# Splitting a buffer fill round the second square root and moving two small steps of a decode kernel

## The chip, the cores and the metric

The kernel runs on one core of a Trainium2 chip. The metric is device time in microseconds. A profile's span (first to last instruction) is 1.3 to 1.6 us shorter than the measured time of the same run.

Names of the profile: PE does matrix products (PEld is its loading of weights), DVE vector work, ACT activation functions, POOL memsets here, and SP issues the loads. PSUM is the memory that PE writes to. A line of a timeline has start and length in us, engine, source line, instruction, what it writes and reads, shapes, count, and in brackets the idle time before it with what ended it. A landing record is the time at which a load's semaphore tells that one of the 16 transfer engines is done with it.

## The reference

One decode step: four batch rows, width 448, 16 query heads on 8 key/value heads, 8192 cached positions of 256. The attention is gated by a small MLP whose output goes through silu. Cut to what matters:

```python
xn = _layernorm(x)
s  = attention(xn, k_cache, v_cache, wq, wo)   # caches: 4 x 8 x 8192 x 256, bf16, read once
xn2 = _layernorm(xn)                           # second layernorm: inside the MLP
# (with one position per row the four shifted groups are zero, so w1 and w2 drop out)
h2 = _gelu(xn2 @ w3) @ w4
return x + s * _silu(xn + h2)
```

The two caches are 268 MB of the 279 MB that are read.

## The kernel before

The work is a loop over 16 pairs of (row, key head). In each round PE turns keys (K), DVE and ACT copy them out of PSUM, PE forms scores, and the value product (PV) of the *previous* pair is done at the end of the round. Round 0 has no previous pair, so its PV runs on a value buffer that must hold finite numbers. At the start that buffer carries the weights wq and w3, and ACT fills what they leave free with zeros:

```python
def prog_act(act):
    ...
    for k, col in ((1, 0), (2, 8)):                  # the two layernorms' square roots
        act.wait_ge(S["v_w"], k)
        c(act.activation(st[:, col + 2:col + 3], st[:, col + 1:col + 2], ACT.Sqrt))
    act.wait_ge(S["g_c"], NPC)                       # POOL's memsets, of pT too
    for t in (vflat[1][:, DK * HDH:NCH * DH], vflat[0][:, DK * FH:NCH * DH]):
        c(act.activation(t, pT[:, 0:1].broadcast_to([P, t.shape[1]]), ACT.Copy))
    act.wait_ge(S["v_w"], 3)
    c(act.activation(gel_b[:, :], gel_a[:, :], ACT.Tanh))
```

DVE then waits for that tanh and ends gelu, before it copies any keys. All loads go through SP's queue. It asks for the next keys when a half of the key buffer has been copied out:

```python
if i > 0:
    sp.wait_ge(S["v_k"], NVK * (i - 1) + 1 + t)
```

At the end the last pair's values come in five pieces and wo's last heads in four. PE's order there:

```python
for i in range(NPIECE - ND):                 # value pieces 0, 1, 2
    take(pe, "dvl%d" % i, 16)
    ins = f_pv(kv, PIECES[i], PIECES[i + 1], pb)
ins.then_inc(S["p_pv"], 1)
take(pe, "v_a")
for i in range(NDG):                         # o's first sums
    pe.matmul(o_ps[i * PQ:(i + 1) * PQ, 0:DQ], selb[:, :],
              ou_f[:, i * DQ:(i + 1) * DQ], start=True, stop=False)
f_direct(NPIECE - ND)                        # piece 3
take(pe, "v_po")
...                                          # sums of pieces 0 to 2, piece 4
take(pe, "dwl0", 16)
f_o(LATE[0])                                 # then the other wo pieces, each when it lands
```

## Time and profile before

| | before |
|---|---|
| median of the first 3 runs | 653.08 us (652.23 to 653.20) |
| span of the profiled run | 651.4 us |
| PE, DVE, ACT busy | 77%, 40%, 41% |
| the queue's transfers | 278.99 MB, 99.5% of 16 engines' span |
| last weights (wo) complete | 648.55 us |

One line of the DMA queue's own timeline: when SP asks for the second pair's keys (columns: start, length, the instruction).

```profile
40.08 12.98 SPq L249 DMA_DIRECT2D kn<-in_A_k_cache_dram  x3
```

### The profile page before, as it was taken

Reading aid. Unit: us, or ns where it says so; the run is one execution under the profiler, and the core shown is the slowest. Engines: PE = TensorE matmul, PEld = TensorE weight load, DVE = VectorE, ACT = ScalarE, POOL = GpSimd, SP = SyncE. Lnnn points to the kernel's source line nnn. Section 1 sums busy time; section 2 is a strip of 40 time slices with the busy share of each in tenths; the row PEclk is TensorE's granted clock in tenths of the full one; section 3 lists DMA queues with packets and bytes.
Section 4 is the critical chain, followed back from the end, with each engine's and each line's share of the span. In section 5 each row is a group of like instructions: output and inputs, shape, how many; then the busy total and the mean of one; then the engine's idle time right before and its main releaser. Section 6 shows DMA issues by size and latency. Waiting matters only on the chain. (4 is left out here: it accounts for less than half of the span.)

```text
span 651.4 us, 22029 instructions
## 1 busy us (share of the span) xinstructions
PE 500.4 (77%) x9695; PEld 411.7 (63%) x9695; DVE 257.4 (40%) x507; ACT 268.5 (41%) x360; POOL 3.7 (1%) x18
## 2 busy tenths in 40 slices
PE   2898989685876958589587867969588595958956
PEld 1794969384673938558285764938467393855924
DVE  7343535252452524335153442525245252433511
ACT  3752636163451615436044542616345161543610
POOL 2000000000000000000000000000000000000000
PEclk9587989797996969889698997969789797988978
DMA  9999999999999999999999999999999999999997
GB/s 385 439 419 430 431 439 441 427 447 423 440 447 404 461 408 457 412 435 453 412 450 417 457 423 425 441 429 445 425 441 447 404 457 412 461 408 435 453 405 301
DMA packets 10641, 279.13 MB, mean 429 GB/s; under 512 B 1028, under 2 KB 3080, under 8 KB 3592
## 3 DMA queue, kind: packets, MB, share of 16 engines
q1 hardware_dynamic: 10616, 278.99, 99.5%
q8 instruction: 7, 0.11, 0.1%
q14 instruction: 2, 0.02, 0.0%
q10 hardware_dynamic: 16, 0.01, 0.0%
HBM read 278.99 MB, written 0.00 MB: 428 GB/s over the span
## 5 line engine op out<-in xcount | busy, mean ns | idle before, releaser
L651 PE MATMUL pst<-ident_b,kn 128*128 128x128 bf16 x4096 | 304.2, 222 | 26.5 <-PEq L317 24.9
L351 ACT ACTIVATE kT<-pst 128x1024 bf16<-128x1024 bf16 x224 | 226.1, 1023 | 119.1 <-ACTq L317 118.9
L349 DVE COPY kT<-pst 128x1024 bf16<-128x1024 bf16 x288 | 197.5, 691 | 175.4 <-DVEq L317 175.3
L651 PEld LDWEIGHTS pst<-ident_b,kn 128*128 128x128 bf16 x4096 | 241.2, 99 | 28.0 <-issue 28.0
L664 PE MATMUL psc<-qc,kT 128*128 128x4 bf16 x4096 | 174.5, 165 | 7.9 <-PEq L317 7.8
L664 PEld LDWEIGHTS psc<-qc,kT 128*128 128x128 bf16 x4096 | 154.4, 97 | 36.6 <-issue 36.1
L696 PE MATMUL psv<-vb,pT 128*8 128x512 bf16 x1024 | 102.3, 497 | 95.6 <-PEq L317 95.6
L372 ACT ACTIVATE pT<-psc,negb 64x128 bf16<-64x128 f32 x64 | 28.4, 535 | 237.2 <-ACTq L317 236.9
L696 PEld LDWEIGHTS psv<-vb,pT 128*8 128x8 bf16 x1024 | 24.6, 93 | 127.4 <-issue 116.5
L507 DVE TENSOR_REDUCE rmax<-psc 64x2 f32<-64x256 f32 x32 | 13.5, 423 | 134.4 <-DVEq L317 134.2
L689 PE MATMUL psm<-sel,po 128*128 128x4 f32 x136 | 19.2, 264 | 1.4 <-PEq L317 1.4
L689 PEld LDWEIGHTS psm<-sel,po 128*128 128x128 f32 x136 | 18.1, 204 | 1.5 <-issue 1.5
L372 ACT ACTIVATION_READ_ACCUMULATOR pT<-psc,negb 64x1 f32 x64 | 16.4, 256 | 0.0
L536 DVE COPY po<-psv 128x512 f32<-128x512 f32 x17 | 11.8, 692 | 9.5 <-DVEq L317 9.5
L528 DVE COPY negb<-psm 128x4 f32<-128x4 f32 x16 | 2.6, 162 | 28.3 <-DVEq L317 28.3
L517 DVE TENSOR_REDUCE gmax<-psm 2x2 f32<-2x128 f32 x16 | 4.5, 279 | 20.2 <-DVEq L317 20.2
L361 ACT ACTIVATE vb<-pT 128x2048 bf16<-128x2048 bf16 (+1 forms) x2 | 10.4, 5252 | 0.0
L677 PEld LDWEIGHTS psm<-diag,ones_f 2*128 2x128 f32 x32 | 4.7, 182 | 7.0 <-issue 7.0
L673 PEld LDWEIGHTS psm<-ident_f,rmax 128*2 128x2 f32 x16 | 1.3, 81 | 11.6 <-issue 11.6
L596 PE MATMUL pst<-ident_b,xn_b 4*128 4x4 bf16 x14 | 0.7, 162 | 9.6 <-DVE xn_b L421 9.5
L596 PEld LDWEIGHTS pst<-ident_b,xn_b 4*128 4x128 bf16 x14 | 0.5, 100 | 10.5 <-issue 9.5
L681 PE MATMUL psw<-rowsum,ones_f 128*128 128x4 f32 x34 | 6.8, 269 | 0.0
(93 smaller groups left out, 84.7 us busy)
## 6 DMA issues: line engine op xcount, KB each, us to landing
kn<-in_A_k_cache_dram SPq DMA_DIRECT2D x30, 4096.0 KB, 26.4
kn<-in_A_k_cache_dram SPq DMA_DIRECT2D x4, 2048.0 KB, 15.6
vb<-in_A_v_cache_dram SPq DMA_DIRECT2D x2, 4096.0 KB, 19.1
kn<-in_A_v_cache_dram SPq DMA_DIRECT2D x1, 4096.0 KB, 27.7
vb<-in_A_wq_dram SPq DMA_DIRECT2D x1, 3584.0 KB, 11.4
kn<-in_A_v_cache_dram SPq DMA_DIRECT2D x1, 2048.0 KB, 26.2
wo_sb<-in_A_wo_dram SPq DMA_DIRECT2D x1, 2016.0 KB, 40.9
vb<-in_B_w_dram SPq DMA_DIRECT2D x1, 1568.0 KB, 14.0
```

What stands on the lines that cost most here:

```text
L349: engine.tensor_copy(dst, src).then_inc(S["v_ev"], 1)
L351: engine.activation(dst, src, ACT.Copy).then_inc(S["a_ev"], 1)
L361: c(act.activation(t, pT[:, 0:1].broadcast_to([P, t.shape[1]]), ACT.Copy))
L372: ins = act.activation(pT[own, 0:NC2 * NR].rearrange("p (c n) -> p n c", n=NR)[:, n], psc[own, 0:NC2 * NR].rearrange("p (c n) -> p n c", n ...
L507: ins = v.tensor_reduce(rmax[own, :], psc[own, 0:NC2 * NR].rearrange("p (c n) -> p n c", n=NR)[:, t * REP:(t + 1) * REP], AX.X, ALU.max)
L536: v.tensor_copy(po[:, :], psv[:, 0:CP * DH]).then_inc(S["v_po"], 1)
L651: ins = pe.transpose(dst[:, n * P:(n + 1) * P], kn[:, t, GC * j + kl, half * P:(half + 1) * P], ident_b[:, :])
L664: ins = pe.matmul(psc[:, kk * NR:(kk + 1) * NR], kT[:, j % RING, n * P:(n + 1) * P], qc[:, :, half, :], start=(half == 0), stop=(half == N ...
L677: pe.matmul(psm[:, P:P + NR], ones_f[0:REP, :], diag[:, :], start=True, stop=True).then_inc(S["p_m2"], 1)
L681: pe.matmul(psw[:, 0:NR], ones_f[:, :], rowsum[:, :], start=True, stop=True).then_inc(S["p_s"], 1)
L689: ins = pe.matmul(psm[:, o:o + NR], po[:, i * DH + dh:(i + 1) * DH:NHALF], sel[:, i, 0:NR], start=(i == 0), stop=(i == CP - 1))
L696: ins = pe.matmul(psv[o:o + CP * NR, 0:CP * DH], pT[:, kk * NR:(kk + CP) * NR], src[:, kk:kk + CP, :].rearrange("p c d -> p (c d)"), start ...
```

## The change

The intent is to free ACT earlier, so that key copies start earlier, and to shorten PE's tail. It has three parts: the fill is split, with 5000 columns put in the idle gap between the square roots; gelu's end moves from the start into the half-time step of the MLP; o's first sums go from behind value piece 2 to behind piece 0. The semaphore that lets PE use the value buffer is now raised by ACT's fill. The core of the diff:

```diff
+            fills = ([vflat[0][:, DK * FH:DK * FH + FILL]],
+                     [vflat[0][:, DK * FH + FILL:NCH * DH], vflat[1][:, DK * HDH:NCH * DH]])
             for k, col in ((1, 0), (2, 8)):
                 act.wait_ge(S["v_w"], k)
                 c(act.activation(st[:, col + 2:col + 3], st[:, col + 1:col + 2], ACT.Sqrt))
-            act.wait_ge(S["g_c"], NPC)
-            for t in (vflat[1][:, DK * HDH:NCH * DH], vflat[0][:, DK * FH:NCH * DH]):
-                c(act.activation(t, pT[:, 0:1].broadcast_to([P, t.shape[1]]), ACT.Copy))
+                act.wait_ge(S["g_c"], NPC)
+                for t in fills[k - 1]:
+                    f = act.activation(t, pT[:, 0:1].broadcast_to([P, t.shape[1]]), ACT.Copy)
+            f.then_inc(S["dv"], 32)
 ... (DVE: the two steps behind "wait_ge(a_c, 5)" move to the head of f_mlp; its own
      sem_inc(dv, 32) goes; later counts on a_c are 2 lower) ...
                 for i in range(NPIECE - ND):
                     take(pe, "dvl%d" % i, 16)
                     ins = f_pv(kv, PIECES[i], PIECES[i + 1], pb)
+                    if i == 0:
+                        take(pe, "v_a")
+                        for n in range(NDG):
+                            pe.matmul(o_ps[n * PQ:(n + 1) * PQ, 0:DQ], selb[:, :],
+                                      ou_f[:, n * DQ:(n + 1) * DQ], start=True, stop=False)
                 ins.then_inc(S["p_pv"], 1)
-                take(pe, "v_a")
-                for i in range(NDG):
-                    pe.matmul(o_ps[i * PQ:(i + 1) * PQ, 0:DQ], selb[:, :],
-                              ou_f[:, i * DQ:(i + 1) * DQ], start=True, stop=False)
                 f_direct(NPIECE - ND)
```

More of the change, by code (lines that the diff above doesn't have):

```diff
@@ L130, in bass_recurrent_scan__gqa_block_cached__mixer_s_mlp__decode_kernel @@
     ROW_PAD = 192
+    FILL = 5000
     TW = NHALF * REP
@@ L459, in prog_dve @@
             v.sem_inc(S["v_po"], 1)
-            v.sem_inc(S["dv"], 32)
             v.wait_ge(S["g_c"], NPC)
@@ L483, in prog_dve @@
                           ).then_inc(S["v_q"], 1)
-            v.wait_ge(S["a_c"], 5)
-            c(v.tensor_scalar(gel_b[:, :], gel_b[:, :], 1.0, 0.5, op0=ALU.add, op1=ALU.mult))
-            c.sync()
-            v.tensor_tensor(hT[:].rearrange("p k a b -> p (k a b)"), gel_b[:, :], gel_u[:, :], ALU.mult
-                            ).then_inc(S["v_hT"], 1)
-            def f_mlp():
+            def f_mlp():
+                v.wait_ge(S["a_c"], 3)
+                v.tensor_scalar(gel_b[:, :], gel_b[:, :], 1.0, 0.5, op0=ALU.add, op1=ALU.mult
+                                ).then_inc(S["v_s"], 1)
+                take(v, "v_s")
+                v.tensor_tensor(hT[:].rearrange("p k a b -> p (k a b)"), gel_b[:, :], gel_u[:, :],
+                                ALU.mult).then_inc(S["v_hT"], 1)
                 take(v, "p_h2")
@@ L575, in prog_dve @@
             f_rz()
-            v.wait_ge(S["a_c"], 6)
+            v.wait_ge(S["a_c"], 4)
             c(v.tensor_scalar(sg4[:, :], sg4[:, :], 1.0, 0.5, op0=ALU.add, op1=ALU.mult))
```

## The prediction

> **What bounds the kernel now.** I read the page first (its busy shares, the slices, the queues), then the stretches around start and end, then the DMA queue's own timeline, then the engines' timelines at both ends. The page's slices and queue rows:
>
> ```profile
> DMA  9999999999999999999999999999999999999997
> q1 hardware_dynamic: 10616, 278.99, 99.5%
> ```
>
> The reader is to see that the transfers are busy in every slice while PE has 77% of the span, DVE 40% and ACT 41%. All data goes through one queue, 278.99 MB. To see whether the queue is ever short of work, I cut the span into stretches (columns: length, busy time of PE, PEld, DVE, ACT, POOL, clock, DMA share, GB/s):
>
> ```profile
> 0.00:2.00 2.00, 0.00 (x0) 0.00 (x0) 0.66 (x2) 0.90 (x1) 0.88 (x8) 1.00 0.92 229
> 2.00:20.00 18.00, 7.01 (x95) 4.32 (x95) 12.26 (x56) 8.38 (x5) 2.80 (x11) 0.96 0.97 412
> 20.00:24.00 4.00, 3.57 (x32) 3.33 (x32) 0.55 (x4) 3.98 (x2) 0.00 (x0) 0.50 1.04 442
> 24.00:40.00 16.00, 14.32 (x212) 14.35 (x213) 5.86 (x11) 7.33 (x9) 0.00 (x0) 0.53 0.98 413
> 40.00:60.00 20.00, 18.10 (x339) 12.97 (x339) 8.32 (x16) 7.06 (x7) 0.00 (x0) 0.83 1.03 431
> ...
> 648.60:651.40 2.80, 0.50 (x7) 0.22 (x4) 0.77 (x2) 0.00 (x0) 0.00 (x0) 1.00 0.01 1
> ```
>
> The DMA share is 0.97 to 1.04 from 2 us on, also at 20 to 24 us, where ACT is filling and PE is about to stall. From the transfer records I also summed the engines at work in every single microsecond: from 2 to 646 us it is never below 15 of 16. There is no hole to close. The DMA queue's own timeline shows the steady state:
>
> ```profile
> 491.06 11.28 SPq L249 DMA_DIRECT2D kn<-in_A_k_cache_dram  x2
> 516.23 0.33 SPq L249 DMA_DIRECT2D vb<-in_A_v_cache_dram  x1
> 529.74 11.27 SPq L249 DMA_DIRECT2D kn<-in_A_k_cache_dram  x2
> ```
>
> A pair starts every 529.74 - 491.06 = 38.68 us for four times 4096 KB, 16.78 MB, or 433.7 GB/s. Compute has time over in each such round; in the list of waits PE waits for values (the psv product) 97.4 us in 15 rounds, 6.5 us a round. What ends the span is the last rows of the timeline:
>
> ```profile
> 648.09 0.41 PEld L742 LDWEIGHTS pst<-wo_sb,OT_all 128*32 128x32 bf16 x8 [0.56 <-issue]
> 648.12 0.97 PE L742 MATMUL pst<-wo_sb,OT_all 128*32 128x224 bf16 x12 [0.37 <-PEq L317]
> 648.66 0.22 PEld L742 LDWEIGHTS pst<-wo_sb,OT_all 128*32 128x32 bf16 x4 [0.16 <-issue]
> 649.13 0.38 DVE L586 TENSOR_TENSOR res<-pst,sg 64x224 f32<-64x224 f32 x1 [2.90 <-PE pst L742]
> ```
>
> By the trace's landing records the last but one piece of wo is complete at 647.99 us and the last at 648.55. PE is idle before both, its loads starting 0.10 us after each. So the time is: about 1 us until the first data moves, 647 us of transfers without a hole, and 2.85 us of fixed work (651.40 - 648.55: four products, two DVE steps of 0.38 us, the store). The measured 653.08 is 1.3 to 1.7 us more than the profiled span.
>
> **What the Trainium skill says.** "DMA: Bandwidth & Descriptors", section "Specifications", gives a fabric ceiling of 435 GB/s beside an HBM limit of about 358 GB/s for one core. The trace agrees with the first (433.7) and not with the second as a bound for this run. There is nothing left in the rate. "ScalarE: Activation LUTs", section "Table sets: the hidden batching unit", says that copy is a filler in every set, so a copy between two square roots should need no new table. The trace agrees for the order it has: the fill starts at 12.31 us, straight after the second square root, without a load, and the only later load is the one ahead of tanh. Section "What ACT_TABLE_LOAD costs" gives about 1283 ns for the load; the trace has 1283 ns, with tanh starting 0.02 us after it, so no further drain shows here. It stays one load after the change.
>
> **Part 1, the fill split.** ACT's timeline at the start:
>
> ```profile
> 6.95 0.20 ACT L358 ACTIVATE st<-st 4x1 f32<-4x1 f32 x1 [4.56 <-DVE st L407]
> 12.21 0.20 ACT L358 ACTIVATE st<-st 4x1 f32<-4x1 f32 x1 [5.06 <-DVE st L407]
> 12.31 10.41 ACT L361 ACTIVATE vb<-pT 128x2048 bf16<-128x2048 bf16 x2
> 22.74 1.28 ACT L363 ACT_TABLE_LOAD   x1
> 24.04 0.25 ACT L363 ACTIVATE gel_b<-gel_a 128x56 f32<-128x56 f32 x1
> 24.31 1.02 ACT L351 ACTIVATE kT<-pst 128x1024 bf16<-128x1024 bf16 x1
> ```
>
> ACT idles 5.06 us between the roots and then fills for 10.41. By shape, 2048 columns take 1891 ns and 10112 take 8612, so 0.834 ns a column and 184 ns fixed. The first 5000 columns take 184 + 5000 x 0.834 = 4.35 us. They may start when POOL has ended its memsets (6.25 + 0.97 = 7.22 us) and end near 11.6, 0.6 us ahead of the second root at 12.21, which isn't delayed. The rest, 5112 and 2048 columns, takes 4.45 + 1.89 = 6.34 us: end at 18.65. Table load to 19.93, tanh to about 20.2 (its input is ready at 19.55 + 0.22 = 19.77). So ACT is free near 20.2 instead of 24.29. One more instruction, 0.18 us, lies in idle time.
>
> **Part 2, gelu's end to half time.** DVE now waits 3.73 us for tanh (24.32) before it empties the first score buffers at 24.84. Two instructions (0.19 + 0.22 us) and that wait leave the start. PE's first keys are turned from 20.11 to 23.68 us, at half clock 0.9 us a group of eight. DVE then empties group 0 near 21.1, ACT group 1 near 22, and PE's first score products can follow at 23.7 where they now start at 25.68: PE gains **2.0 us** there, no more, because the turning of keys becomes what it waits for. The next keys, asked for at 40.08 us, are asked for near 38. But the queue isn't empty at 40.08: the transfer ahead of it, wo, is complete on its first engine at 42.43 us and on its last at 44.51. A longer queue moves no byte sooner. **Worth on the span: 0.** At half time PE's half-way product has to wait for the two steps, some 0.6 us once. In steady rounds PE has 6.5 us over, and the next transfer is asked for over 20 us before it lands: also 0. (The residual copies already lie at half time in the old kernel; only gelu's end moves.)
>
> **Part 3, o's first sums ahead.** Four products of 352 ns, overlapped to 0.55 us, leave the stretch after the third value piece and go behind the first. There PE has idle time:
>
> ```profile
> 642.80 0.34 PEld L696 LDWEIGHTS psv<-kn,pT 128*8 128x8 bf16 x10 [2.26 <-issue]
> 643.26 0.33 PEld L772 LDWEIGHTS pst<-ou_f,selb 128*32 128x32 f32 x4
> 643.79 0.69 DVE L536 COPY po<-psv 128x512 f32<-128x512 f32 x1 [5.66 <-DVEq L317]
> 644.05 0.48 PEld L752 LDWEIGHTS pst<-pT,kn 128*128 128x128 bf16 x16 [0.46 <-issue]
> 644.60 1.02 PEld L778 LDWEIGHTS pst<-sel,po 128*128 128x128 f32 x8
> ```
>
> PE stands still about 2 us before the third piece (642.80), so 0.55 us fits there. But after it the L778 products need DVE's copy, which ends at 643.79 + 0.69 = 644.48 whichever way; they can't move. The L752 piece lands at 643.94 and starts at 644.05 already. So PE gains under 0.1 us by 645.85, and the wo pieces at 647.99 and 648.55 swallow that. **Worth: 0.**
>
> Sum: 0 + 0 + 0, with the median of before at 653.08 and its runs from 652.23. I take **652.9 us**, the middle of what these runs would give again, leaning a little low for the longer queue.
>
> **Rivals.** *The start counts in full:* if some executions that weren't profiled have a hole near 40 us (the queue has only 2.35 us left on its first engine there, and a first byte takes about 1 us), the earlier request would be worth up to 2.0 us: 651.1. For it: the margin is small, and before spreads over 1 us. Against it: no hole in the trace, and the profiled run is as slow as the others. *The end counts in full:* PE's tail shortens by 0.55 us, 652.5. Against it: PE is idle before both last pieces. *Slower, a new wait:* the first fill outlasts the gap and holds the second root, hence xn2 and the start of w3's products. It would have to be 0.6 us late to be felt at all, and some 4 us late to empty the queue at 40 us; or the half-time steps cost more than the 6.5 us that a round has over. Either would make 653 to 654. *The rate of the transfers changes* with a deeper queue or with ACT writing at another time: no term for it in the trace; 1 us either way.
>
> **Range and chances.** Three of the rivals lie within 2 us and the runs of one kernel within 1 us, so 651.2 to 654.4. Faster by 2% is 640 us, less than the bytes take at 433.7 GB/s (278.99 / 0.4337 = 643.3 us, plus 1 and 2.85 at the ends); only another count of bytes could do that. Slower by 2% needs 13 us of holes. Chances 0.01, 0.98, 0.01.
>
> **What would show it.** Right: the first fill of 4.35 us lies between the roots, tanh starts near 20, the first score products near 23.7, the second pair's keys are asked for near 38 instead of 40.08, and yet the rounds stay 38.68 us, the DMA share stays near 1 throughout and the last wo piece lands within 1 us of 648.55. L772 stands before 642.8 and L778 stays where it is. Wrong: the last landing moved by more than 1 us, or a microsecond with fewer than 15 engines at work in either kernel, or PE not idle before the last two wo pieces.

## The result, and the profile after

| | before | after |
|---|---|---|
| median of 6 runs each | 652.77 us (652.23 to 653.20) | 653.05 us (652.84 to 653.65) |
| ratio, 95% interval | | 1.0005 [0.9992, 1.0018]: same |
| profiled span | 651.4 us | 651.3 us |
| second pair's keys asked for | 40.08 us | 33.94 us |
| first score product | 25.68 us | 23.58 us |
| last wo piece complete | 648.55 us | 648.41 us |

The page's slices and queue rows of the changed kernel, and two of the stretches (columns as in the prediction):

```profile
DMA  9999999999999999999999999999999999999997
q1 hardware_dynamic: 10616, 278.99, 99.5%
```

```profile
2.00:20.00 18.00, 7.02 (x95) 4.33 (x95) 12.22 (x55) 12.67 (x8) 2.79 (x11) 1.00 0.96 409
20.00:24.00 4.00, 3.79 (x42) 3.82 (x43) 1.97 (x7) 1.28 (x3) 0.00 (x0) 1.00 1.03 438
```

Nothing moved for the transfers: the same bytes, the same share. (The share of a stretch counts a packet where it starts, so it can pass 1. The clock column reads 1.00 wherever the profile holds no clock record. The first record stands at 15.1 us in the kernel before and at 26.1 in this one, so the 1.00 of the second line is no measurement: the first 32 key products took 3.57 us in both kernels.) What moved is beside the transfers. Between 2 and 20 us ACT is busy 12.67 us instead of 8.38, and between 20 and 24 us 1.28 instead of 3.98, because part of the fill went into its gap. Its timeline at the start:

```profile
6.98 0.20 ACT L361 ACTIVATE st<-st 4x1 f32<-4x1 f32 x1 [4.60 <-DVE st L411]
7.29 4.37 ACT L364 ACTIVATE vb<-pT 128x5000 bf16<-128x5000 bf16 x1
12.25 0.20 ACT L361 ACTIVATE st<-st 4x1 f32<-4x1 f32 x1 [0.60 <-DVE st L411]
12.36 6.24 ACT L364 ACTIVATE vb<-pT 128x5112 bf16<-128x5112 bf16 x2
18.62 1.28 ACT L367 ACT_TABLE_LOAD   x1
19.92 0.25 ACT L367 ACTIVATE gel_b<-gel_a 128x56 f32<-128x56 f32 x1
22.20 1.02 ACT L352 ACTIVATE kT<-pst 128x1024 bf16<-128x1024 bf16 x1 [2.03 <-ACTq L318]
```

The reader is to see the second line, the fill between the roots, with 0.60 us of idle time left behind it, and the last line's wait of 2.03 us: ACT now stands ready for keys that PE hasn't turned yet. The SP request that answers to the 40.08 us of before:

```profile
33.94 16.74 SPq L250 DMA_DIRECT2D kn<-in_A_k_cache_dram  x3
```

It comes 6.14 us earlier and then waits in a longer queue. By the landing records that load of keys completes at 54.17 us on its last engine, and did so at 54.16 us before. The end of the changed kernel, after two lines of the kernel before for comparison:

```profile
642.83 0.81 PE L696 MATMUL psv<-kn,pT 128*8 128x512 bf16 x10 [1.78 <-PEq L317]
645.85 1.90 PE L742 MATMUL pst<-wo_sb,OT_all 128*32 128x224 bf16 x32
```

```profile
642.69 0.81 PE L700 MATMUL psv<-kn,pT 128*8 128x512 bf16 x10 [0.93 <-PEq L318]
643.65 0.69 DVE L540 COPY po<-psv 128x512 f32<-128x512 f32 x1 [5.26 <-DVEq L318]
643.91 0.48 PEld L756 LDWEIGHTS pst<-pT,kn 128*128 128x128 bf16 x16 [0.91 <-issue]
644.46 1.02 PEld L783 LDWEIGHTS pst<-sel,po 128*128 128x128 f32 x8
647.99 0.97 PE L746 MATMUL pst<-wo_sb,OT_all 128*32 128x224 bf16 x12 [0.38 <-PEq L318]
```

PE's wait ahead of the third piece shrank from 1.78 to 0.93 us. Its wait ahead of the last wo pieces is what it was, 0.38 us (0.37 before).

### The profile page after: what moved, and what is told of

Its sections match the earlier page's. It is cut to its first block, busy times and chain, and to the rows that moved or that the text cites. A ratio compares the mean times of both kernels' runs of the same rounds, so it can differ in the third digit from the quotient of the medians.

```text
span 651.3 us, 22030 instructions
## 1 busy us (share of the span) xinstructions
PE 501.3 (77%) x9695; PEld 409.0 (63%) x9695; DVE 257.2 (39%) x507; ACT 268.7 (41%) x361; POOL 3.7 (1%) x18
## 5 line engine op out<-in xcount | busy, mean ns | idle before, releaser
L700 PE MATMUL psv<-vb,pT 128*8 128x512 bf16 x1024 | 105.1, 506 | 99.6 <-PEq L318 98.7
L364 ACT ACTIVATE vb<-pT 128x5000 bf16<-128x5000 bf16 (+2 forms) x3 | 10.6, 3568 | 0.1
## 6 DMA issues: line engine op xcount, KB each, us to landing
wo_sb<-in_A_wo_dram SPq DMA_DIRECT2D x1, 2016.0 KB, 40.8
```

What stands on the lines that cost most here:

```text
L364: f = act.activation(t, pT[:, 0:1].broadcast_to([P, t.shape[1]]), ACT.Copy)
L700: ins = pe.matmul(psv[o:o + CP * NR, 0:CP * DH], pT[:, kk * NR:(kk + CP) * NR], src[:, kk:kk + CP, :].rearrange("p c d -> p (c d)"), start ...
```

## The experiments

The theory to be tested: the 279 MB in the queue set the time, the start of compute counts only if it lets the queue run dry, and PE's tail counts only beyond the idle time that it holds. The rivals: the start counts in full and something later gives it back; the tail counts in full; or compute sets the time and the change simply did nothing to it. In the runs below "before" was timed again in the same rounds: median 652.70 us for the first four, 652.77 for the next four, 652.80 for the last three.

### Each half of the change alone

```diff
 # e1_start_only: after.py with o's first sums back behind piece 2
 # e2_sums_only:  before.py with o's first sums behind piece 0
```

> Parts 1 and 2 alone (fill split, gelu's end at half time; o's first sums at their old place). Theory (the transfers set the time): ratio 1.000 within 0.002, last landing within 0.3 us of 648.5, although the second pair's keys are asked for 2 to 6 us before 40.08. Rival (the start counts and something later gives it back): 651 or 647, since the part that gives it back is not in this kernel.

> Part 3 alone (o's first sums behind the first value piece, start as in the old kernel). Theory: ratio 1.000 within 0.002; PE idle grows by about 0.5 us ahead of the fourth value piece and not at the end. Rival (PE's tail sets the end): 0.55 us less, 652.2. Also a second look at the old start: if half clock up to 38 us follows from PE's pause near 24 us, it is seen again here and not in the run of the start alone.

Measured: 652.88 us, ratio 1.0003 [0.9986, 1.0019], and 652.75 us, ratio 1.0000 [0.9984, 1.0017]. The start alone asked for the second pair's keys at 34.04 us and its last wo piece was complete at 648.37. So the sums don't give a gain back, since they aren't in that kernel. The half-time step still is in it, but it can't be what gives the gain back either: the load that was asked for 6 us earlier was complete at 54.03 us, against 54.16 before, and half time comes after 320 us. The gain was never one for the span. For the sums alone the times don't decide: the interval also holds the rival's 0.55 us less (0.9992). In the trace they gave nothing: the last wo piece was complete at 648.49 and PE's last wo product ended at 649.03 (648.55 and 649.09 before).

That trace also shows what I had not expected. By the clock records PE was at half clock from 635.1 to 641.9 us, where the kernel before has 636.3 to 639.8. It came to the wo products at 646.49 instead of 645.85 and did all 44 in 2.54 us without a wait. So how much PE has over at the end differs from run to run; in this one it was next to nothing.

### Bytes: half of one pair's values left out

```diff
 # e6_less_v: after.py with
-                    load(vv, src, 0, NC2, "dv")
+                    load(vv, src, 0, NCH if i == NPAIR - 2 else NC2, "dv")
```

This kernel is wrong: the second half of one pair's values is the pair before's. The check passed it all the same ("correct": true on record), so that check doesn't notice half of one pair's values.

> The changed kernel without the second half of the values of the last but one pair (wrong result on purpose): 4.194 MB less in the queue. Theory: 4.194 MB / 433.7 GB/s = 9.67 us less, 643.3. Rival (compute or a chain of waits sets the time): 653.

Measured: 643.31 us, ratio 0.9857 [0.9842, 0.9872], 9.46 us less than before (9.74 less than the changed kernel's 653.05). The queue's row of its page:

```profile
q1 hardware_dynamic: 10616, 274.80, 99.4%
```

With the compute untouched, the time follows the bytes at 4.194 MB / 9.46 us = 443 GB/s, 0.21 us short of the 9.67 that the steady rate gives. This shows directly what the profile's share suggested, and the rival of a compute bound falls.

### A later start: when does it begin to cost?

Extra fills of 5000 columns hold ACT, and with it the key copies. A semaphore of their own keeps the overlapping writes in order.

```diff
 # e3_old_fill1 (n = 1), e4_old_fill3 (n = 3): before.py, ahead of its fills
+            for i in range(n):
+                t = vflat[0][:, DK * FH:DK * FH + 5000]
+                act.activation(t, pT[:, 0:1].broadcast_to([P, t.shape[1]]), ACT.Copy).then_inc(S["xf"], 1)
+                act.wait_ge(S["xf"], i + 1)
 # e5_new_fill3 (n = 3), e9_new_fill1 (n = 1): after.py, the same behind its fills
```

> The old kernel with one more fill of 5000 columns ahead of its fills: ACT is free about 4.45 us later. Theory: a late start costs only the hole that it makes in the queue, request of the second pair's keys + 1.0 us to first data - 43.5 (mean end of the wo transfer over the engines). Request at 40.5 to 44.5, by PE's clock: cost 0 to 2.0 us, 652.8 to 654.8. Rival (the start counts in full): 4.45 us more, 657.2.

> The old kernel with three more fills of 5000 columns: ACT is free about 13.3 us later. Theory: request at 48 to 53.5, a hole of 5.5 to 11 us, 658 to 664, and the measured addition equals request + 1.0 - 43.5 within 0.7 us. Rival (the start counts in full): 666.1. Rival (start never counts): 652.8.

> The changed kernel with the same three more fills, behind its own: tanh would come near 33.3, the first ACT copy of keys near 33.5 instead of 22.2, 11.3 us later. Theory: request at 45 to 49, hole 2.5 to 6.5, 655.5 to 659.5, again request + 1.0 - 43.5 within 0.7 us; and 2 us or more below the old kernel with three more fills, so here, with the queue run dry, the change's start does count. Rival (start counts in full): 664.3. Rival (it never counts): 652.8.

> The changed kernel with one more fill of 5000 columns behind its own. The three runs with a hole put the knee at a request near 40.8 us (their profiled spans grew by request - 40.8, within 0.1). Here the first ACT copy of keys comes near 24.6 instead of 22.2, so the request for the second pair's keys comes at 36 to 40, short of the knee. Theory: 0 to 0.2 us more, 653.0, where the same fill in the old kernel cost 3.2. Rival (every us of a late start counts): 2.4 us more, 655.4.

| kernel | request | idle of the queue, 41 to 52 us | profiled span, and growth | median of runs (range) |
|---|---|---|---|---|
| before | 40.08 | 0 | 651.4 | 652.77 |
| before + 1 fill | 44.32 | 2.73 | 654.9, +3.5 | 655.86 (653.86 to 656.52) |
| before + 3 fills | 49.18 | 7.49 | 659.9, +8.5 | 665.67 (661.43 to 665.85) |
| after | 33.94 | 0 | 651.3 | 653.05 |
| after + 1 fill | 35.43 | 0 | 652.0, +0.7 | 653.11 (652.88 to 653.56) |
| after + 3 fills | 47.79 | 6.09 | 658.3, +7.0 | 659.11 (657.19 to 660.00) |

All in us; the idle time is the sum over the 16 engines divided by 16, from the transfer records. The request and the hole in the old kernel with one more fill, from the queue's timeline and from the stretches:

```profile
44.32 12.21 SPq L249 DMA_DIRECT2D kn<-in_A_k_cache_dram  x3
```

```profile
42.00:44.00 2.00, 2.00 (x42) 2.00 (x41) 0.89 (x2) 1.02 (x1) 0.00 (x0) 1.00 0.45 167
44.00:46.00 2.00, 1.69 (x47) 1.61 (x45) 0.94 (x2) 0.00 (x0) 0.00 (x0) 1.00 0.64 198
```

The same two stretches of the old kernel as it is:

```profile
42.00:44.00 2.00, 2.00 (x48) 2.00 (x46) 1.40 (x3) 1.77 (x2) 0.00 (x0) 1.00 1.30 533
44.00:46.00 2.00, 2.00 (x53) 2.00 (x51) 1.18 (x2) 1.48 (x3) 0.00 (x0) 1.00 0.92 395
```

The column before the last is the DMA share: 0.45 and 0.64 where the old kernel has 1.30 and 0.92. PE is busy 2.00 and 1.69 us against 2.00 and 2.00; the queue shows the loss far more. The mechanism holds: a lost microsecond of the queue never comes back in the following 600 us. The idle time makes up 2.73 of 3.5, 7.49 of 8.5 and 6.09 of 7.0 us. Most of the rest is transfers that took longer: summed over all records and divided by 16 they took 0.9, 1.0 and 0.6 us more than in the same kernel without extra fills. The size was off. I expected a growth of request + 1.0 - 43.5, that is 1.8, 6.7 and 5.3 us within 0.7, and found 3.5, 8.5 and 7.0: about 1.7 us more in each, a miss of my own stated width. For the kernel with one more fill three terms account for 1.5 of the 1.7. The wo data ended at 42.78 us in the mean and not at 43.5 (its landing records have 43.13 in that run, and a landing record comes some 0.35 us behind the data): 0.72. The first data followed the request by 0.96 to 1.80 us, by engine, 1.34 in the mean and not 1.0: 0.34. And each engine's first transfer after the hole took up to 1.94 us instead of 1.213, together 0.41. The remaining 0.2 I can't assign. What the runs say is simpler: the growth is the request less 40.8 us (3.5, 8.4 and 7.0). Carried back to no growth, which no run tests between 40.08 and 44.32, this line puts the old kernel's request at 40.08 only 0.7 us short of costing something.

The change moved it to 33.94. With one more fill the old kernel lost 3.2 us in the median and the changed one 0.06 over itself; with three, 665.67 stands against 659.11. **The change bought slack where there was no lack.** The ratios to before are 1.0037 [1.0018, 1.0055] and 1.0195 [1.0178, 1.0212] for the old kernel, 1.0004 [0.9989, 1.0019] and 1.0090 [1.0074, 1.0106] for the changed one; only the second is unclear at 2%, the others are the same. The old kernel's two medians lie above the ranges that I had stated. The other four runs of "before + 3 fills" lie 4 us above its profiled one (661.43), at what the rival of a full count had said (666.1). No profile shows their requests, so why is open, and in that row only the profiled run has request and span both known. What speaks against the full count is "after + 1 fill", where the same fill cost 0.06 us in the median. The +0.7 of "after + 1 fill" is no hole: the profiled run was that kernel's slowest, and its other runs had spans of 651.3 to 651.8. Its last wo piece was complete 0.28 us later than in the changed kernel. The rest is PE's tail: PE was at half clock from 636.3 to 643.1 us (637.1 to 640.5 in the changed kernel), came to the wo products at 647.21 instead of 645.71 and did all 44 in one piece of 2.48 us. There PE set the end, without any work added to the tail.

### A heavier tail at both places

More copies of o's first sums, into a PSUM bank that nothing reads:

```diff
 # e7_sums4_late, e10_sums9_late: before.py; e8_sums4_early, e11_sums9_early: after.py
+                for m in [*range(NDG)] * n:          # n = 3 or 8
+                    pe.matmul(pst[2][m * PQ:(m + 1) * PQ, 0:DQ], selb[:, :],
+                              ou_f[:, m * DQ:(m + 1) * DQ], start=True, stop=True)
```

> The old kernel with three more copies of o's first sums at their old place, into a bank that nothing reads: 1.65 us more for PE behind the third value piece. Theory (PE has about 0.4 us over before the last wo pieces): 1.2 us more, 654.0. Rival (tail counts in full): 1.65. Rival (nothing of PE's tail counts): 0.

> The changed kernel with the same three copies at the new place, behind the first value piece. Theory: PE's idle time of 0.9 to 1.3 us ahead of the third piece and 0.4 us before the last wo pieces takes nearly all: 0 to 0.9 us more, 0.3 as worked out, so about 0.9 us below the old place. That is what the move is worth when the tail is heavy. Rival (place does not matter): the same as at the old place.

> As the run of three more copies at the old place, with eight: 4.4 us more for PE. With three, the median grew by 0.7 and the profiled span by 1.07 for 1.65 us of products, so PE had 0.6 to 0.9 us over. Theory: 3.5 to 3.8 us more, 656.2 to 656.6. Rival (nothing of PE's tail counts): 652.8.

> As the run of three more copies at the new place, with eight. Theory: PE's idle time ahead of the third, the fourth and the last wo pieces takes 0.9 + 0.4 + 0.4 = 1.7 us of 4.4 us: 2.7 us more, 655.5, about 1 below the old place. Rival (the place does not matter): 3.5 to 3.8 us more, as at the old place.

Measured with three: 653.48 us at the old place, ratio 1.0009 [0.9996, 1.0023], and 653.05 at the new one, ratio 1.0010 [0.9996, 1.0024]. Both are the same at 2%, both intervals hold 1. With eight: 654.60 us, ratio 1.0031 [1.0017, 1.0045], and 654.23 us, ratio 1.0024 [1.0010, 1.0037]. PE's tail does count once it is 3 us longer, but for only half of what I had said (1.8 and 1.4 instead of 3.5 to 3.8 and 2.7). The timeline of the eight copies at the old place shows why:

```profile
643.68 3.20 PE L775 MATMUL pst<-ou_f,selb 128*32 128x224 f32 x32
646.81 0.47 PEld L752 LDWEIGHTS pst<-pT,kn 128*128 128x128 bf16 x16 [0.36 <-issue]
648.46 2.48 PE L742 MATMUL pst<-wo_sb,OT_all 128*32 128x224 bf16 x44
```

The copies took 3.20 us, not 4.4: one block of four costs 0.40 us in a row, where the single block shows 0.55 with its end. The 44 wo products ran in one piece of 2.48 us; in the kernel before they stretch from 645.85 to 649.09, 3.24 us, so 0.76 us of that was waiting. The wo products start at 648.46 instead of 645.85, 2.61 us later, and 2.61 - 0.76 = 1.85 us is the growth of the span (653.2 against 651.4). The last wo piece was complete 0.16 us earlier here (648.39), so PE had about 1.2 us over behind the third value piece (3.20 - 1.85 - 0.16), more than the 0.55 us that the change takes out of there. That is an estimate from one pair of profiles; where PE was longer at half clock, as in the runs of the sums alone and of "after + 1 fill", there was less.

Whether the early place is worth anything in a heavy tail stays open. The medians with eight copies differ by 0.37 us, less than the intervals can separate, and PE's clock differed in the profiled runs (the first value piece's 32 products took 1.90 us in one and 3.46 in the other), which moves the whole tail.

## Why the prediction was right

The time, 653.05 us, lies 0.15 us from the predicted 652.9, and the class is the predicted one. The runs of one kernel spread over 1 us, so that the distance is so small is luck; that nothing is gained is not. By its steps:

- **The bound.** Right, and shown: leaving bytes out took 9.46 us of the predicted 9.67; no microsecond of the changed kernel between 2 and 646 us has fewer than 15 of 16 engines at work.
- **Part 1.** First fill 4.37 us (predicted 4.35), second root at 12.25, not delayed (12.21 before), tanh at 19.92 (19.93). One table load behind the fills, as said.
- **Part 2, the step with a wrong size.** The first score products came at 23.58 us as worked out (23.7). But "the next keys, asked for at 40.08 us, are asked for near 38" was off: it was 33.94. The term left out is PE's speed afterwards. In the stretches below (before, then after; the clock stands ahead of the last two columns), PE is busy throughout in both and does 59 matmuls in one and 88 in the other:

```profile
28.00:32.00 4.00, 4.00 (x59) 4.00 (x56) 1.36 (x2) 2.05 (x2) 0.00 (x0) 0.50 0.94 406
```

```profile
28.00:32.00 4.00, 4.00 (x88) 4.00 (x85) 1.84 (x4) 2.48 (x3) 0.00 (x0) 1.00 0.99 422
```

  The clock records have PE on half clock from 28 us at the latest until 37.5 to 39.0 us in the four profiles with the old start and no delay added; with the new start full clock begins at 22.9 to 26.1 us. This wasn't chance: between 28 and 36 us the score products' weight loads took 114 to 119 ns in those four profiles, and 96 to 97 ns in all six with the new start (the one with one more fill included). What in the start decides it, no run here isolates. It cost nothing either way. (The "first score buffers" that the prediction has at 24.84 us hold turned keys: its line is `kT<-pst`.)
- **The margin of the queue.** The prediction put it at 2.35 us less about 1 us for the first byte. The runs with a hole put it at 0.7 us, by their line carried back. The rival "the start counts in full" was thus closer than I had thought, though no profile of the unchanged kernel crossed the line.
- **The half-time wait.** Predicted 0.6 us once, for nothing in the span. In the lists of waits PE's MLP product waits 1.3 us before and 1.9 after.
- **Part 3.** Right: the products fitted into PE's wait ahead of the third piece, and L783 stayed tied to DVE's copy. PE came to the wo products at 645.71 instead of 645.85, but the fourth value piece had landed 0.14 us earlier too (643.80, 643.94), so the move's own share is about 0. That the rest would have been swallowed is argued from the 1.2 us that PE had over by the eight copies. The step behind it, that PE is idle before both last pieces, holds in the profiles of both kernels. It doesn't hold in every run: in that of the sums alone and that of "after + 1 fill" PE did its 44 wo products without a wait.

No version among these beats the kernel before, and the experiments point to none: only fewer bytes moved the time down.

## What to carry to other kernels

Where one queue is busy in every microsecond, work out first how far each request stands from letting it run dry; engine time that you free ahead of that point is slack, not speed. A late request costs its whole hole for good, so slack can be worth having, but it shows only once something else makes the start late. Test such a bound by leaving bytes out and by delaying on purpose: both give a slope, where a null result gives none.

## What the Trainium skill lacked or had wrong

- "TensorE: Matmul & The Clock Gate", section "What's actually happening", has PE leave half clock after about 3.4 us of sustained work. The kernel before had PE busy 4.00 of 4.00 us from 28 to 32 us and again from 32 to 36 us, and its clock record has 0.50 from 18.5 to 39.0 us; the old kernel with three more sums has the same (18.5 to 38.9). Why is open.
- "DMA: Bandwidth & Descriptors", section "Where 436 GB/s comes from", says that for loads from HBM the HBM side binds, at about 358 GB/s. With one core at work the steady rounds here moved 433.7 GB/s. The sentence lacks a condition that the same page gives under "Measured (HBM→SBUF, 128 partitions, SWDGE, issued from GpSimd)": about 358 GB/s is for both cores of a pair streaming.
- The same page, section "Specifications", gives about 0.6 us to the first byte for this kind of queue. Where the queue had run dry, the first data came 0.96 to 1.84 us after the request, and an engine's first transfer took up to 2.07 us instead of 1.213, by the transfer records of the three runs with a hole.
- "ScalarE: Activation LUTs", section "What ACT_TABLE_LOAD costs", adds a drain of about 1380 ns to a load. Here the load of 1283 ns began 0.02 us after the last fill and tanh 0.02 us after the load, before and after the change, so no drain shows on either side.
